# Where a chunk's mask, a few stage slots and one block's logits stand in a gated linear attention with an MLP behind it

## The chip, the cores and the metric

The kernel runs on one core of a Trainium2 chip. The metric is device microseconds of one execution; lower is better. Five runs of the kernel before gave 628.28, 629.21, 629.96, 630.31 and 630.61 us: a median of 629.96 us. One further execution was profiled and took 628.72 us; all rows below come from it.

## The reference

Inputs are q, k, v and f_logit of shape (4, 8, 768, 48), and two weight matrices; all in fp32 but the weights, which arrive as 64-bit floats and are rounded on the core.

```
f = sigmoid(f_logit)
for t in range(768):
    state = f[t][:, None] * state + outer(k[t], v[t])     # 48 x 48 for each batch and head
    y[t]  = q[t] @ state
x = y, as (4*768, 8*48)
h = x @ w_in                                              # 384 -> 2048
out = (h * erf(softplus(h))) @ w_out                      # 2048 -> 384
```

## The kernel before

**Chunks and blocks.** The 4 x 768 tokens are cut into 24 chunks of 128 tokens (numbered from 0; six to a batch), and two chunks make a block of 256 tokens. For each chunk the attention has four stages:

- `stage_d(g)`: one product (line 358) sums the chunk's log gates along time; ScalarE takes two exponentials of it (361 and 364), SyncE sends four small DMAs with the chunk's total decay into `Tall` (line 367, for chunks from 3 on), and VectorE scales q and k (371, 375).
- `stage_t(g)`: q and k are transposed by TensorE (385) and copied out by ScalarE (391, 393).
- `stage_s(g)`: if the chunk is not the last of its batch, `state` makes the products of k and v (433, into the bank `dS`) and VectorE adds the old state (446) and multiplies by `Tall` (449; for a batch's first chunk the one step 442). Then come the score products of k and q (414) and VectorE's mask, one pass of 128 x 1024 (419), whose output is `A`.
- `stage_y(g)`: `y_matmuls` (146) multiplies `A` with v and q with the state that the chunk *before* left; ScalarE copies the result into `xT` (462).

Before a block's stages `prepare` turns its logits into logs: VectorE clips them (335), ScalarE does an Exp and an Ln (339, 340). The Exp and Ln live in another table set than the Tanh of the activation, so a change of set costs ScalarE a table load.

**The MLP.** `hidden` makes the first product (line 515, four tiles of 12 products to a block and group), ScalarE copies it out (522), `activate` runs in steps on ScalarE (152, 155, 487) and VectorE (160, 489). `project` makes the second product by a scheme of seven products for each 2 x 2 of tiles (645) whose sums VectorE prepares (543), and puts the output rows together with a copy (661) and adds (653). `round_piece` turns each of 16 pieces of the weights from 64 bits into fp32: one ScalarE pass (285) and six VectorE passes (287, 291, 296, 300, 305, 310). A piece of `w_in` must be rounded before the products that read it.

**What sets the order.** Every engine runs its instructions in the order in which the program lists them. The list is a loop over turns `it`, one turn for each block; in a turn the generator `slots(it)` yields after each MLP product, and at slot `s` other work is put in: the stages at the slots of the list `at`, steps of the weights' rounding (`weights_step`, one a slot in turn 0 up to slot 42), of the activation, loads, and `prepare`. So a stage's place in `at` decides what stands ahead of it on all five engines. Chunks 0 to 2 run ahead of the loop; turn 0 holds the stages of chunks 3 to 5, turn 1 those of chunks 6 and 7.

**Buffers that bind.** `dS`, the transposes, `ps_d` and `y` share one PSUM pool of two banks (tag `at`): the next of them waits until the last reader of the bank is done. The scores have a bank pair of their own with one buffer.

Of the kernel before, what the change touches and what calls it, by code (L numbers as in the profile page):

```python
# [67 lines left out]
P = 128  # L68
# [3 lines left out]
def kernel(  # L72
# [20 lines left out]
    NCH = S // P  # L93
# [12 lines left out]
    def fixed(name, shape, dtype=FP32, pool=const):  # L106
        return pool.tile(shape, dtype, name=name)
# [58 lines left out]
    fix = main.enter_context(tc.tile_pool(name="fix", bufs=1))  # L166
# [23 lines left out]

    NS, NA = 3, 3
    S_WORDS = NS * NA * FG // 2 * P
    scratch = fixed("scratch", [P, S_WORDS + 7 * DH], pool=fix)
    sums_sb = scratch[:, 0:S_WORDS].rearrange("p (b n j t) -> p b n j t", b=NS, n=NA, j=FG // 2)
    rows_sb = scratch[:, S_WORDS:].rearrange("p (n c) -> p n c", n=7)

    def w_sums(gi):
        return wT[:, gi, :].rearrange("p (n j c) -> p n j c", n=NT, j=FG // 2)
# [197 lines left out]

    def stage_s(g):
        b, c = divmod(g, NCH)
        qT, kT = qTs[g], kTs.pop(g)
        if g in totals:  # L400

            pairs = dps[g % 2][:].rearrange("t (a r) d -> t a (r d)", r=2)
            for a in range(HP):
                nc.tensor.matmul(
                    totals[g][:, a : a + 1], lhsT=pairs[:, a, :], rhs=ident[:, P - 1 : P],
                    start=True, stop=True,
                )
            nc.vector.tensor_copy(out=Tall[:, g, :], in_=totals.pop(g))
        if c < NCH - 1:
            state(g, c)  # L410
        sc = ps_sc.tile([P, 2, HP, P], FP32, name="sc", tag="sc")
        for a in range(HP):
            for r in range(2):
                nc.tensor.matmul(  # L414
                    sc[:, r, a, :], lhsT=kT[rows(r), a, :], rhs=qT[rows(r), a, :],
                    start=True, stop=True,
                )
        A = work1.tile([P, 2, HP, P], FP32, name="A", tag="A")
        nc.vector.tensor_tensor(  # L419
            out=A[:].rearrange("s r a t -> s (r a) t"),  # L420
            in0=sc[:].rearrange("s r a t -> s (r a) t"),
            in1=tri[:].unsqueeze(1).broadcast_to((P, H, P)),
            op=ALU.mult,
        )
        As[g] = A

    def state(g, c):
        dS = ps_at.tile([P, HP, D], FP32, name="dS", tag="at")
# [185 lines left out]
    def project(blk):  # L614


        ops = [ps_moe.tile([P, 2, 512], FP32, name="ops", tag="moe") for _ in range(2)]
        end = blk == n_blocks - 1
        ops.append(ps_sc.tile([P, 2, 512], FP32, name="ops", tag="sc") if end else ops[1])
        place = {n: ops[i][:, j, k * DH : (k + 1) * DH] for n, (i, j, k) in {  # L620
            1: (0, 0, 0), 2: (0, 1, 0), 6: (0, 1, 1), 5: (1, 0, 0), 7: (1, 0, 1), 3: (2, 1, 0), 4: (2, 1, 1),
        }.items()}
        first = [1, 2, 5, 3]

        def pair(n):
            i, j = {2: (0, 1), 5: (1, 0), 3: (2, 1)}[n]
            return ops[i][:, j, 0 : 2 * DH].rearrange("p (n c) -> p n c", n=2)

        def products(gis, ns):
            for gi in gis:  # L630
                gr = groups[blk, gi]
                while gr["sums"] is None:
                    sum_step()
                a11, a12, a21, a22 = blocks(gr["h"])
                w = w_out_sb[:, FG * gi : FG * (gi + 1), :]
                s, t = gr["sums"], w_sums(gi)
                for j in range(2):
                    w1, w2 = w[:, j, :], w[:, 2 + j, :]
                    for n in ns:
                        x, y = {  # L640
                            1: (a11, w1[:, 0:DH]), 2: (a12, w2[:, 0:DH]), 3: (s[2], w2[:, DH:]),
                            4: (a22, t[:, 3, j, :]), 5: (s[0], t[:, 0, j, :]),
                            6: (s[1], t[:, 1, j, :]), 7: (a21, t[:, 2, j, :]),
                        }[n]
                        nc.tensor.matmul(  # L645
                            place[n], lhsT=x[:, j, :], rhs=y,
                            start=(gi == 0 and j == 0 and n in first),
                            stop=(gi == n_g - 1 and j == 1), skip_group_check=True,
                        )
                        yield  # L650

        def plus(out, x, y):
            nc.vector.tensor_tensor(out=out, in0=x, in1=y, op=ALU.add)  # L653

        o = rows_sb
        yield from products((0, 1), (1, 2, 6))
        yield from products((0,), (5, 7, 3, 4))
        to_sum.appendleft(sum_h(groups[blk, 3]))
        yield from products((1,), (5, 7, 3, 4))
        yield from products((2, 3), (1, 2, 6))  # L660
        nc.scalar.copy(out=o[:, 3, :], in_=place[1])  # L661

        plus(o[:, 0:5:4, :], o[:, 3:4, :].broadcast_to((P, 2, DH)), pair(2))
        def fives():

            plus(o[:, 5:7, :], o[:, 4:5, :].broadcast_to((P, 2, DH)), pair(5))

        yield from products((2, 3), (5, 7))
        if end:

            fives()
            plus(o[:, 3, :], o[:, 5, :], place[7])
        yield from products((2, 3), (3, 4))
        if not end:
            fives()
        plus(o[:, 1:3, :], o[:, 5:7, :], pair(3))
        if not end:
            plus(o[:, 3, :], o[:, 5, :], place[7])
        store(blk)

    def chain(*gens):
# [38 lines left out]
    with tc.manual_schedule():  # L720
# [118 lines left out]
        for it in range(n_blocks):  # L839
            gen, n = slots(it)  # L840
            if it == 0:
                todo = [(stage_d, 3), (stage_t, 3), (stage_s, 3), (stage_y, 3), (stage_d, 4), (stage_t, 4),
                        (stage_d, 5), (stage_s, 4), (stage_t, 5), (stage_y, 4)] + stages(2)[4:]
                at = [3, 10, 15, 22, 28, 36, 42, 47, 56, 74, 77, 82, 87, 93]
            else:
                todo = stages(it + 2) if it + 2 < n_blocks else []
                at = [int(3 + (n - 13) / max(1, len(todo)) * i) for i in range(len(todo))]
            if it + 3 < n_blocks:
                prepare_at = at[todo.index((stage_d, (it + 3) * CPB))] - 14
            at, todo = deque(at), deque(todo)  # L850
            for s, _ in enumerate(gen):
                due += (1 if s < 42 else 0.6 if s < 72 else 0.3) if it == 0 else 0.42 if it == 1 else 0.6
                while due >= 1:
                    weights_step()
                    due -= 1
                if s % 6 == 3:
                    load_more()
                if at and s == at[0]:
                    at.popleft()
                    f, g = todo.popleft()  # L860
                    f(g)
                    if f is stage_y:
                        load_to(g + LOOK)
                if it == 0 and s == 17:
                    prepare(2, 0, CPB)
                if it == 0 and s == 9:
                    load_f(6)
                    load_f(7)
                if s == n // 2 and it + 4 < n_blocks:
                    for j in range(CPB):  # L870
                        load_f((it + 4) * CPB + j)
                if it + 3 < n_blocks and s == prepare_at:
                    prepare(it + 3, 0, CPB)
                if it < 2:
                    step = s % 12 == 6 and (it or s >= 24)
                elif it == 2:
                    step = s % 5 in (1, 3)
                else:
                    step = s % 9 in (2, 6)
                if step:  # L880
                    act_step()
                if it == 2:
                    if s == n - 6:
                        to_sum.extend(sum_h(groups[1, gi]) for gi in range(NS))
                    sum_step()
                elif it > 2:
                    if s == n_o and it < n_blocks - 1:
                        to_sum.extend(sum_h(groups[it - 1, gi]) for gi in range(NS))
                    if it == n_blocks - 1 and s % n_o == 40 and s < 2 * n_o:
                        blk = n_blocks - 2 + s // n_o  # L890
                        to_sum.extend(sum_h(groups[blk, gi]) for gi in range(NS))
                    if s < n_o or s % 3 == 0 or it == n_blocks - 1:
                        sum_step()
                if it == n_blocks - 2 and s in (5, 40):
                    next(check)
            assert not todo
# [214 lines left out]
```

## Time and profile before

| what | value |
|---|---|
| median of five runs | 629.96 us |
| the profiled execution | 628.72 us |
| its span (first to last instruction) | 626.9 us |
| TensorE products, share of the span busy | 97% |
| VectorE | 68% |
| ScalarE | 56% |
| GpSimd | 4% |
| TensorE's granted clock, mean | 0.995 |

How to read the rows: times are microseconds from the span's start. PE is TensorE's products and PEld its weight loads, DVE is VectorE, ACT ScalarE, POOL GpSimd, SP SyncE, which issues the DMAs. A row of the timeline gives start, duration, engine, line, operation, output and inputs, shapes, how many instructions it merges, and in brackets how long the engine had idled and what released it. A row of the waits gives the waiting engine and line, the releaser, the sum, how often, and the longest. A row of the windows gives for each engine the busy time in a stretch, then the granted TensorE clock, the DMA engines' share and the rate.

### The profile page before, as it was taken

To read this page: it belongs to the slowest core of one execution; us is meant where nothing else is said; L and a number is where in the kernel's file an instruction comes from. 1 tells how busy PE (TensorE), PEld (TensorE's weight loads), DVE (VectorE), ACT (ScalarE), POOL (GpSimd) and SP (SyncE) were. 2 spreads that over 40 slices of the span, in tenths; PEclk is the share of its full clock that TensorE was granted. 3 is DMA by queue.
4 is the path that set the end of the run, shared out by engine and by line. 5 is a ranking of instruction groups with operands and counts; after the bars stand their busy time and mean duration, and the time that the engine had idled before them with its cause. 6 is when DMAs were issued, how large, how long until landed. Compare 5 with 4: busy or idle time off the path is not lost.

```text
span 626.9 us, 11233 instructions
## 1 busy us (share of the span) xinstructions
PE 605.3 (97%) x4727; PEld 536.0 (85%) x4727; DVE 428.2 (68%) x651; ACT 351.7 (56%) x419; POOL 25.6 (4%) x24
## 2 busy tenths in 40 slices
PE   8896899899999999999999999999999999999996
PEld 7775788788668989889889989988989989989995
DVE  4899997755899576667566675685594764756751
ACT  5345555658763666665855856756747446556300
POOL 0000000000491000000000000000000000000000
PEclk9998999999999999999999999999999999999999
DMA  9999723310211211311221131031000000000000
GB/s 198 244 279 250 198 69 63 64 35 18 51 38 27 66 38 25 78 24 26 51 54 25 27 77 25 14 84 30 15 26 1 2 27 0 15 13 0 26 26 30
DMA packets 120633, 37.02 MB, mean 59 GB/s; under 512 B 112384, under 2 KB 115456, under 8 KB 120576
## 3 DMA queue, kind: packets, MB, share of 16 engines
q1 hardware_dynamic: 118496, 35.84, 24.7%
q8 instruction: 39, 0.64, 0.4%
q10 hardware_dynamic: 2080, 0.39, 0.4%
q14 instruction: 18, 0.15, 0.1%
HBM read 31.46 MB, written 4.72 MB: 58 GB/s over the span
## 4 chain that ended last, share of the span: by engine, by line
PE 80%; DVE 9%; ACT 6%; DMA 2%; issue 1%; SPq 1%; POOL 0%; DVEq 0%; POOLq 0%; ACTq 0%
PE hps L515 34%; PE ops L645 31%; PE y L146 5%; PE sc L414 3%; PE ps_t L385 3%; PE ps_d L358 2%; ACT x L155 1%; DVE e L160 1%; DMA Tall<-dp 1%; DVE scratch L543 1%; PE dS L433 1%; DVE A L419 1%; DMA lt<-in_f_logit_dram 1%; PE busy L348 1%; ACT e L152 1%
## 5 line engine op out<-in xcount | busy, mean ns | idle before, releaser
L515 PE MATMUL hps<-xT,w_in_sb 128*128 128x256 f32 x1152 | 262.1, 382 | 1.4 <-ACT xT L462 1.3
L515 PEld LDWEIGHTS hps<-xT,w_in_sb 128*128 128x128 f32 x1152 | 215.3, 190 | 36.3 <-issue 3.0
L160 DVE SCALAR_TENSOR_TENSOR e<-x,e 128x1024 f32<-128x1024 f32 x96 | 120.9, 1260 | 26.5 <-ACT x L155 26.4
L155 ACT ACTIVATE x<-Hg,serf_bias 128x1024 f32<-128x1024 f32 x88 | 97.7, 1141 | 0.1
L645 PE MATMUL ops<-wT,Hg 128*128 128x192 f32 x352 | 86.8, 328 | 0.0
L152 ACT ACTIVATE e<-Hg 128x1024 f32<-128x1024 f32 x44 | 46.6, 1059 | 63.2 <-DVE Hg L489 62.8
L522 ACT COPY Hg<-hps 128x1024 f32<-128x1024 f32 x44 | 44.5, 1010 | 62.5 <-PE hps L515 62.5
L489 DVE TENSOR_TENSOR Hg<-Hg,e 128x1024 f32<-128x1024 f32 x44 | 54.2, 1233 | 32.3 <-ACT e L487 32.3
L645 PE MATMUL ops<-wT,scratch 128*128 128x192 f32 x320 | 75.1, 326 | 0.7 <-DVE scratch L543 0.7
L645 PE MATMUL ops<-w_out_sb,Hg 128*128 128x192 f32 x352 | 74.3, 328 | 0.0
L645 PEld LDWEIGHTS ops<-wT,Hg 128*128 128x128 f32 x352 | 61.7, 190 | 2.7 <-issue 0.2
L645 PEld LDWEIGHTS ops<-w_out_sb,Hg 128*128 128x128 f32 x352 | 60.0, 190 | 3.7 <-issue 1.2
L653 DVE TENSOR_TENSOR scratch<-scratch,ops 128x384 f32<-128x384 f32 (+1 forms) x44 | 21.3, 502 | 53.2 <-ACT scratch L661 44.3
L645 PEld LDWEIGHTS ops<-wT,scratch 128*128 128x128 f32 x320 | 55.8, 190 | 1.0 <-POOL wT L543 1.0
L487 ACT ACTIVATE e<-e 128x1024 f32<-128x1024 f32 x48 | 50.5, 1051 | 6.2 <-DVE e L160 6.2
L371 DVE TENSOR_TENSOR qd<-qn,dp 128x384 f32<-128x384 f32 x24 | 13.4, 557 | 50.2 <-ACT dp L361 50.2
L146 PE MATMUL y<-A,vt 128*32 128x128 f32 x768 | 36.2, 281 | 7.5 <-DVE A L419 5.8
L146 PEld LDWEIGHTS y<-A,vt 128*32 128x32 f32 x768 | 27.9, 110 | 14.5 <-DVE A L419 5.2
L645 PE MATMUL ops<-w_out_sb,scratch 128*128 128x192 f32 x160 | 39.1, 326 | 0.0
L419 DVE TENSOR_TENSOR A<-sc,tri 128x1024 f32<-128x1024 f32 x24 | 29.4, 1225 | 2.6 <-PE sc L414 2.1
L146 PE MATMUL y<-qT,Mbd 128*32 128x128 f32 x480 | 31.2, 279 | 0.0
L462 ACT COPY xT<-y 128x384 f32<-128x384 f32 x24 | 11.4, 474 | 30.5 <-PE y L146 30.5
(108 smaller groups left out, 647.8 us busy)
## 6 DMA issues: line engine op xcount, KB each, us to landing
lt<-in_f_logit_dram SPq DMA_DIRECT2D x24, 192.0 KB, 3.9
qn<-in_q_dram SPq DMA_DIRECT2D x24, 192.0 KB, 4.2
out_dram<-scratch SPq DMA_DIRECT2D x12, 384.0 KB, 3.6
kn<-in_k_dram SPq DMA_DIRECT2D x23, 192.0 KB, 4.1
vt<-in_v_dram SPq DMA_DIRECT2D x23, 192.0 KB, 3.0
w_out_sb<-in_moe_w_in_dram SPq DMA_DIRECT2D x4, 768.0 KB, 6.5
Hg<-in_moe_w_in_dram SPq DMA_DIRECT2D x4, 768.0 KB, 6.5
Hg<-in_moe_w_out_dram SPq DMA_DIRECT2D x4, 768.0 KB, 5.6
```

Source lines behind the costliest of these rows:

```text
L146: nc.tensor.matmul(y[M * i : M * (i + 1), kt, :], lhsT=terms[n][0], rhs=terms[n][1], start=(n == 0), stop=(n == len(terms) - 1), skip_grou ...
L152: nc.scalar.activation(out=dst[:], in_=h, func=AF.Exp)
L155: nc.scalar.activation(out=dst[:], in_=h, func=AF.Tanh, bias=serf_bias[:, i : i + 1], scale=SERF_KAB[i][0])
L160: nc.vector.scalar_tensor_tensor(out=e[:], in0=x[:], scalar=SERF_KAB[i][2], in1=e[:], op0=ALU.add, op1=ALU.mult)
L385: nc.tensor.transpose(ps[:, a, :], flat[:, a, :], ident[:])
L419: nc.vector.tensor_tensor(out=A[:].rearrange("s r a t -> s (r a) t"), in0=sc[:].rearrange("s r a t -> s (r a) t"), in1=tri[:].unsqueeze(1) ...
L487: nc.scalar.activation(out=e[:], in_=e[:], func=AF.Tanh, scale=SERF_C)
L489: nc.vector.tensor_tensor(out=h, in0=h, in1=e[:], op=ALU.mult)
L515: nc.tensor.matmul(hps[:, j, :], lhsT=w_in_sb[:, kt, ft * P : (ft + 1) * P], rhs=xTs[blk][:, kt, :], start=(kt == 0), stop=(kt == n_k - 1),)
L522: nc.scalar.copy(out=gr["h"], in_=hps[:])
L645: nc.tensor.matmul(place[n], lhsT=x[:, j, :], rhs=y, start=(gi == 0 and j == 0 and n in first), stop=(gi == n_g - 1 and j == 1), skip_grou ...
L653: nc.vector.tensor_tensor(out=out, in0=x, in1=y, op=ALU.add)
```

## The change

- **Mask ahead of the state** for chunks 0 to 5: `stage_s` issues the scores and the mask first and `state` after them. From chunk 6 on the order stays.
- **Turn 0's slots:** `stage_d(4)` goes from slot 28 to 34, `stage_t(4)` from 36 to 42, `stage_d(5)` from 42 to 47, `stage_s(4)` from 47 to 51, `stage_t(5)` from 56 to 60, `stage_d(6)` from 77 to 76, `stage_s(5)` from 82 to 79, `stage_t(6)` from 87 to 88, `stage_y(5)` from 93 to 94; `stage_y(4)` stays at 74.
- **Logits of block 2** (the third): `prepare(2, 0, CPB)` goes from slot 17 to 25 of turn 0. Eight steps of the weights' rounding now stand ahead of it.
- **Turn 1's slots:** 3, 7, 11, 16, 20, 24, 29, 33 become 2, 6, 11, 17, 25, 29, 34, 41. The logits of block 4 hang 14 slots ahead of `stage_d(8)`, and go with it from slot 6 to 11.
- **Two output rows fewer:** the seven products' sums 5 and 6 go into rows 3 and 4 in place of rows of their own, so `scratch` is 2 x 192 words a partition smaller. In the last block the add of product 7 can no longer be done ahead of the last products: it follows the add of products 3 and 4.

```diff
-    scratch = fixed("scratch", [P, S_WORDS + 7 * DH], pool=fix)
+    scratch = fixed("scratch", [P, S_WORDS + 5 * DH], pool=fix)
...
     def stage_s(g):
         b, c = divmod(g, NCH)
+        late = g >= 6
...
-        if c < NCH - 1:
+        if late and c < NCH - 1:
             state(g, c)
         sc = ps_sc.tile([P, 2, HP, P], FP32, name="sc", tag="sc")
...
         As[g] = A
+        if not late and c < NCH - 1:
+            state(g, c)
...
         def fives():
 
-            plus(o[:, 5:7, :], o[:, 4:5, :].broadcast_to((P, 2, DH)), pair(5))
+            plus(o[:, 3:5, :], o[:, 4:5, :].broadcast_to((P, 2, DH)), pair(5))
...
         if end:
 
             fives()
-            plus(o[:, 3, :], o[:, 5, :], place[7])
         yield from products((2, 3), (3, 4))
         if not end:
             fives()
-        plus(o[:, 1:3, :], o[:, 5:7, :], pair(3))
-        if not end:
-            plus(o[:, 3, :], o[:, 5, :], place[7])
+        plus(o[:, 1:3, :], o[:, 3:5, :], pair(3))
+        plus(o[:, 3, :], o[:, 3, :], place[7])
         store(blk)
...
-                at = [3, 10, 15, 22, 28, 36, 42, 47, 56, 74, 77, 82, 87, 93]
+                at = [3, 10, 15, 22, 34, 42, 47, 51, 60, 74, 76, 79, 88, 94]
             else:
                 todo = stages(it + 2) if it + 2 < n_blocks else []
-                at = [int(3 + (n - 13) / max(1, len(todo)) * i) for i in range(len(todo))]
+                at = [n * x // 48 for x in (2, 6, 11, 17, 25, 29, 34, 41)] if it == 1 else [int(3 + (n - 13) / max(1, len(todo)) * i) for i in range(len(todo))]
...
-                if it == 0 and s == 17:
+                if it == 0 and s == 25:
                     prepare(2, 0, CPB)
```

More of the change, by code (lines that the diff above doesn't have):

```diff
@@ L192 @@
     S_WORDS = NS * NA * FG // 2 * P
-    scratch = fixed("scratch", [P, S_WORDS + 7 * DH], pool=fix)
+    scratch = fixed("scratch", [P, S_WORDS + 5 * DH], pool=fix)
     sums_sb = scratch[:, 0:S_WORDS].rearrange("p (b n j t) -> p b n j t", b=NS, n=NA, j=FG // 2)
-    rows_sb = scratch[:, S_WORDS:].rearrange("p (n c) -> p n c", n=7)
+    rows_sb = scratch[:, S_WORDS:].rearrange("p (n c) -> p n c", n=5)
     def w_sums(gi):
```

## The prediction

> **What bounds the kernel now.** I read the page first, then the windows, then the waits of TensorE, then the timeline around the longest of them.
>
> ```profile
> span 626.9 us, 11233 instructions
> PE 605.3 (97%) x4727; PEld 536.0 (85%) x4727; DVE 428.2 (68%) x651; ACT 351.7 (56%) x419; POOL 25.6 (4%) x24
> ...
> 30.00:45.00 15.00, 14.84 (x142) 12.06 (x135) 14.52 (x21) 6.71 (x10) 0.00 (x0) 1.00 1.05 264
> 45.00:50.00 5.00, 0.68 (x4) 0.25 (x2) 2.92 (x7) 0.00 (x0) 0.00 (x0) 1.00 1.15 327
> 50.00:53.00 3.00, 2.50 (x55) 2.43 (x56) 2.97 (x5) 0.19 (x1) 0.00 (x0) 0.64 0.81 271
> 60.00:100.00 40.00, 38.30 (x316) 32.22 (x315) 38.50 (x56) 23.70 (x31) 0.00 (x0) 1.00 0.48 127
> 200.00:560.00 360.00, 360.00 (x2799) 325.49 (x2798) 234.56 (x359) 221.04 (x251) 0.00 (x0) 1.00 0.15 32
> ...
> PE y L146 <- DVE A L419: 5.8, 2, 4.8
> PE ps_t L385 <- DVE Sn L446: 2.7, 2, 1.7
> PE y L146 <- ACT qT L391: 1.7, 1, 1.7
> ```
>
> TensorE is busy without a gap from 200 to 560, so nothing is to be had there: what the change can move lies before 200 and at the very end. In 30 to 100 TensorE and VectorE are both nearly full (14.52 of 15 and 38.50 of 40 for VectorE), because VectorE rounds the weights there; a VectorE that runs late is then as dear as a TensorE that waits. The waits name three places: `y` for the mask (4.8 at 45, 1.0 at 28), a transpose for a state's read (1.7 at 74, 1.0 at 196), `y` for a copy of qT (1.7 at 110).
>
> ```profile
> 45.77 0.34 DVE L446 TENSOR_TENSOR Sn<-dS,Mbd 48x192 f32<-48x192 f32 x1
> 48.07 0.35 DVE L449 TENSOR_TENSOR Mbd<-Sn,Tall 48x192 f32<-48x192 f32 x1 [1.97 <-DMA Tall<-dp]
> 49.22 1.23 DVE L419 TENSOR_TENSOR A<-sc,tri 128x1024 f32<-128x1024 f32 x1
> 50.36 0.95 DVE L305 SCALAR_TENSOR_TENSOR Hg<-Hg 128x768 f32<-128x768 uint32 x1
> 50.50 0.32 PE L146 MATMUL y<-A,vt 128*32 128x128 f32 x4 [4.82 <-DVE A L419]
> 52.22 0.56 DVE L335 TENSOR_SCALAR lt<-lt 128x768 f32<-128x768 f32 x1
> 58.02 0.81 PE L358 MATMUL ps_d<-lt,tri 128*128 128x384 f32 x2
> ...
> 106.39 0.84 ACT L339 ACTIVATE lt<-lt 128x768 f32<-128x768 f32 x1 [2.65 <-DVE lt L335]
> 108.11 1.28 ACT L155 ACT_TABLE_LOAD   x1
> 112.15 0.58 ACT L391 COPY qT<-ps_t 128x512 f32<-128x512 f32 x1
> 112.78 0.43 PE L146 MATMUL y<-A,vt 128*32 128x128 f32 x8 [1.67 <-ACT qT L391]
> ...
> 618.38 0.94 DVE L653 TENSOR_TENSOR scratch<-scratch,ops 128x384 f32<-128x384 f32 x2 [1.70 <-PE ops L645]
> 620.98 0.56 DVE L653 TENSOR_TENSOR scratch<-scratch,ops 128x384 f32<-128x384 f32 x1 [1.66 <-PE ops L645]
> ```
>
> The reader is to see that chunk 3's state waits for the decay's DMA with the mask behind it; that `y(3)` does not need that state (it takes the state of chunk 2); that qT's copy at 112 stands behind block 4's logits; and that the last block ends on one add of 0.56.
>
> **The change, part by part.**
>
> *Chunks 0 to 2, mask first.* Today VectorE works on the state beside the score products. In chunk 1 the state runs 20.27 to 21.76, the scores 20.15 to 21.31, the mask 21.80 to 23.03. Turned round, the scores take the place of the state's products (19.66 to 20.82), the mask runs 20.85 to 22.08 and the state, 1.49 less an overlap of 0.08, to 23.45: VectorE is 0.42 later. Chunk 2 costs the same. In chunk 0 the state is 0.72 long and its bank is freed after it, at 15.0, where the k transpose started at 14.57: 0.3 to 0.4. So VectorE, which feeds the weights to line 515, comes to chunk 3 late by 0.3 + 0.42 + 0.42 = 1.1. Bounds: 0, and 3.5, three whole score products of 1.16 uncovered. I take 1.1 since the rows of chunk 1 give it directly. `y(2)` loses its 1.0 of waiting for the mask, but the products behind it wait for rounded pieces (0.3 and 0.2 at 37.9 and 42.7), so this gain is spent on VectorE's lateness.
>
> *Chunk 3.* The mask starts when the state does today, 45.77 + 1.1 = 46.9, and ends at 48.1. The decay landed at 47.95, so the 1.97 wait is gone: the mask fills it. VectorE's own work between 45.77 and 50.36 is 4.59 - 1.97 = 2.62, so line 305 starts at 46.9 + 2.62 = 49.5 instead of 50.36: VectorE leads by 0.85. TensorE starts `y(3)` at 48.15 instead of 50.50. The half clock also goes: 50 to 53 shows 0.64, and `y(3)` took 50.50 to 53.36, 2.86 where `y(4)` took 1.69. But today's product after it waits for ScalarE's copy of xT till 55.76, behind the logits on ScalarE, so part of that was hidden.
>
> *Logits of block 2 and `stage_d(4)`.* Ahead of line 335 now stand a whole piece (287 at 52.69 to 287 at 57.33: 4.64) and two passes (57.33 to 58.51: 1.18). So it starts at 52.22 - 0.85 + 4.64 + 1.18 = 57.2. Today the end of line 340 comes 2.31 after its start (52.22 to 54.53), so `ps_d(4)` starts at 59.55. TensorE gets there with 35 products of line 515 done, where it has 29 today: six of 0.432, 2.59. It has nothing to do from about 55.6 (48.15, `y` 1.69, copy 0.6, twelve products 5.2): it waits 4.0. Against today at equal work: 59.55 - (58.02 + 2.59) = -1.06.
>
> A new wait of 4.0 may bring the half clock back, as the 4.82 did: by that row it costs 0 to 1.17. I take 0, since in the next step TensorE waits 1.7 again, and what it loses to the clock it would otherwise wait. The Trainium skill, "TensorE: Matmul & The Clock Gate", Part 1, says that after an idle window of about 3.4 us the array runs at half clock until a busy window has passed; that speaks against this new wait, and worked from its figure it is an estimate of up to 1.7 us lost, with which the sum would be +0.5 instead of the one below.
>
> *`stage_t(4)`, `stage_d(5)`, `stage_s(4)`, `stage_t(5)`.* dp(4) follows on ScalarE, and VectorE's scaling (371) now stands behind a full piece after line 335: from 57.65, 4.64 + 2.58 (58.51 to 61.09, line 296 to the end of 305) = 64.85, so the transpose starts at 65.35 with 43 products done; today 62.12 with 37. Equal work: 65.35 - (62.12 + 2.59) = +0.64, so the lead is given back. Then the k transpose of chunk 5 needs chunk 4's state read (the 1.7 wait, second read at 75.85 to 76.21). Ahead of that read now stand the mask (1.15) and two passes more (300 and 305, 1.5): 76.21 + 2.65 - 0.85 = 78.0, with 61 products done against 57 at 76.36 today (four: 1.73). Equal work: 78.1 - 78.09 = 0. So at `y(4)`, slot 74 in both, the opening nets 0.0. Bounds: -1.06 (the lead at `ps_d(4)` is kept) and +2.4 (3.5 late in place of 1.1).
>
> *Queues passed.* On SyncE two transfers of w_out's raw pieces (768 KB, landing after about 5.6) now go ahead of chunk 4's four decay transfers, and block 4's two logit loads ahead of chunk 8's. Chunk 4's decays landed at 63.50 today and are read at 75.49; 12 us cover them. Without that cover each piece would cost about 2.2. GpSimd gets nothing.
>
> *Turn 1.* Today ScalarE does lines 339 and 340 (106.39 to 108.11), a table load of 1.28 and two more passes before qT(7) at 112.15; the `y` of chunk 6 needs the bank that this copy frees. Now the logits stand at slot 11, behind the transposes of the same slot, so the copies come first. The 1.74 of idle goes (110.51 to 112.78, of which 0.53 is the product's own). What is late next is the copy of xT before the products that follow, 0.2. Net -1.55; bounds -1.74 and 0 (the same copy late behind another pass). ScalarE gets two table loads more, 2 x 1.28; it idles 2.65, 1.36, 1.02 and 2.98 between 103 and 122, which covers them; uncovered they cost 2.56 on an engine that has 36 us free in this hundred.
>
> *The end.* The last add becomes two, as at 618.38: 0.94 instead of 0.56, +0.38 on the path to the last store. Bounds 0.27 and 0.41. The smaller scratch and the reuse of rows 3 and 4 change no instruction's size: 0.
>
> Sum: 0.0 - 1.55 + 0.38 = -1.17. The profiled execution, 628.72, becomes 627.55. It lies 1.24 under the median of the runs, so I put the difference on the median: 629.96 - 1.17 = 628.8.
>
> **Rivals.**
> 1. *The opening keeps its gain.* If ScalarE and VectorE serve chunk 4 without the wait of 1.7 for its transpose, the 1.06 stays: 629.96 - 2.23 = 627.7. For it: today this transpose waits for nothing (62.12). Against: VectorE's queue, full in 60 to 100.
> 2. *Turn 1's wait only moves.* Another ScalarE pass stands ahead of the copy: 0.0 + 0.0 + 0.38 gives 630.3. For it: ScalarE's queue is what made the wait; against: 64 of 100 us busy.
> 3. *Slower: the state's bank is held behind the mask.* In chunks 1 and 2 the bank of `dS` comes free 1.23 later each, and transposes, `y` and `ps_d` need it: 2.46 if nothing covers it, 628.8 + 2.46 = 631.25. For it: 1.7 at 74 is just such a wait. Against: in chunk 1 `y` comes at 23.61 and the bank is free at about 23.2. It decides once VectorE reaches chunk 3's mask later than 46.9 + 2.4 = 49.3.
>
> **How the numbers follow.** A measurement of this kernel tells about 0.2%, 1.26 us, from no change. The sum of -1.17 stands just inside that. Chances: forecast 0.51 (0.21 beyond 1.26, 0.29 within, 0.01 slower), rival 1 0.23 (all faster), rival 2 0.12 (all same), rival 3 0.14 (0.13 slower, 0.01 same). Together faster 0.44, same 0.42, slower 0.14. The range, 626.9 to 631.2, runs from rival 1 with turn 1 and the last add at their bounds (627.7 - 0.19 - 0.11 = 627.4), less 0.5 for a median of runs that spread over 2.3, to rival 3, 631.2.
>
> **What would show it.** In the profile after: no wait of 4.8 for the mask, `y(3)` near 48, and a clock of 1.00 in 50 to 53; line 335 near 57 and `ps_d(4)` waiting some 4 us for line 340; a transpose waiting 1.7 near 64 for line 371; no wait of `y` for qT near 111; a last pair of adds of 0.94. I am wrong if VectorE idles again between 30 and 76, if the clock falls after the wait at 56 and `y(4)` starts later than 85.7, or if the early chunks lose more than 1.1.

## The result, and the profile after

The changed kernel took 628.79 us (median of 32 runs, 627.98 to 630.13) beside 629.52 us of the kernel before (median of 55 runs, 628.12 to 631.16). The ratio is 0.9989, with a 95% interval from 0.9984 to 0.9995: 0.7 us faster, between 0.3 and 1.0. The forecast was 628.8 us with a gain of 1.17; the gain is real, inside the 0.2% that I had called no change, and about half a microsecond smaller than the sum. That the two times agree to 0.01 us is luck: the five runs that the forecast stood on had a median of 629.96, 0.44 above the 629.52 of the 55, and the gain by the medians, 0.73, is 0.44 below the 1.17.

Lines moved in the changed file. Line 414 is now 415, 419 is 420, 433 is 436, 446 is 449, 449 is 452, 462 is 465, 515 is 518, 522 is 525, 582 is 585, 645 is 648, 653 is 656; lines up to 391 keep their numbers. The runs below that hold the edit of `stage_s` have the new numbers too. First the page's head and the windows of the opening (start and end, length, busy time and count of PE, PEld, DVE, ACT and POOL, then clock, DMA share, GB/s):

```profile
span 626.2 us, 11238 instructions
...
45.00:50.00 5.00, 3.52 (x65) 2.79 (x63) 4.80 (x9) 0.17 (x1) 0.00 (x0) 1.00 1.11 333
50.00:53.00 3.00, 3.00 (x17) 2.32 (x14) 2.90 (x5) 1.49 (x2) 0.00 (x0) 1.00 1.11 302
53.00:60.00 7.00, 3.09 (x14) 2.37 (x13) 6.79 (x10) 2.10 (x3) 0.00 (x0) 1.00 0.98 262
60.00:65.00 5.00, 5.00 (x16) 3.82 (x15) 4.83 (x8) 4.64 (x7) 0.00 (x0) 0.66 0.58 220
```

TensorE's idle time has moved from 45 to 50 into 53 to 60, and with it the half clock, from 50 to 53 into 60 to 65. VectorE is busy 4.80 of 5 where it was busy 2.92. The waits of TensorE between 30 and 130 in the changed kernel (who waits, for whom, sum, times, longest):

```profile
PE ps_d L358 <- ACT lt L340: 3.9, 1, 3.9
PE y L146 <- DVE A L420: 1.5, 1, 1.5
PE ps_t L385 <- DVE Sn L449: 1.0, 1, 1.0
PE hps L518 <- DVE w_in_sb L310: 0.7, 1, 0.7
PE ps_t L385 <- DVE qd L371: 0.7, 1, 0.7
```

The wait of 4.8 for the mask is 1.5, the wait for qT is gone, and the new wait of 3.9 for the logits is there. The two waits of 0.7 stand at 39.79 and 37.46, at chunk 3, and not at chunk 4. The timeline of the changed kernel at the steps of the prediction:

```profile
47.06 1.22 DVE L420 TENSOR_TENSOR A<-sc,tri 128x1024 f32<-128x1024 f32 x1
48.34 0.42 PE L146 MATMUL y<-A,vt 128*32 128x128 f32 x8 [1.48 <-DVE A L420]
48.58 0.35 DVE L452 TENSOR_TENSOR Mbd<-Sn,Tall 48x192 f32<-48x192 f32 x1
57.28 0.55 DVE L335 TENSOR_SCALAR lt<-lt 128x768 f32<-128x768 f32 x1
59.64 1.33 PE L358 MATMUL ps_d<-lt,tri 128*128 128x384 f32 x2 [3.91 <-ACT lt L340]
60.77 4.93 PE L518 MATMUL hps<-xT,w_in_sb 128*128 128x256 f32 x16
65.53 0.60 PE L385 MATMUL ps_t<-ident,qd 128*128 128x128 f32 x4
78.30 0.63 PE L385 MATMUL ps_t<-ident,kd 128*128 128x128 f32 x4 [1.00 <-DVE Sn L449]
84.91 0.42 PE L146 MATMUL y<-A,vt 128*32 128x128 f32 x8
619.15 0.49 PE L648 MATMUL ops<-wT,Hg 128*128 128x192 f32 x2
619.67 0.94 DVE L656 TENSOR_TENSOR scratch<-scratch,ops 128x384 f32<-128x384 f32 x2 [2.05 <-PE ops L648]
620.64 0.37 SPq L585 DMA_DIRECT2D out_dram<-scratch  x1
```

The last products and the last store of the kernel before, beside the last three of these rows:

```profile
620.45 0.49 PE L645 MATMUL ops<-wT,Hg 128*128 128x192 f32 x2
621.56 0.37 SPq L582 DMA_DIRECT2D out_dram<-scratch  x1
```

| step | before | forecast | after |
|---|---|---|---|
| chunk 3's mask starts | 49.22 | 46.9 | 47.06 |
| `y(3)` | 50.50 | 48.15 | 48.34 |
| line 335 of block 2 | 52.22 | 57.2 | 57.28 |
| `ps_d(4)`, and its wait | 58.02, 0 | 59.55, 4.0 | 59.64, 3.91 |
| transposes of chunk 4 | 62.12 | 65.35 | 65.53 |
| k transpose of chunk 5 | 76.36 | 78.0 | 78.30 |
| `y(4)` | 84.69 | 84.7 | 84.91 |
| last add (after: the last pair) | 620.98 | | 619.67 |

The last store is issued at 620.64 where it was 621.56: 0.92 earlier, made of +0.22 at `y(4)`, -1.52 from there to the start of the last products, and +0.38 behind it. So the pair of profiles comes near the forecast; the medians of many runs give less. That remainder, and which of the parts earns, is what the experiments were for.

### The profile page after: what moved, and what is told of

It reads as the page before. It is cut to its first block, busy times and chain, and to the rows that moved or that the text cites. A ratio compares the mean times of both kernels' runs of the same rounds, so it can differ in the third digit from the quotient of the medians.

```text
span 626.2 us, 11238 instructions
## 1 busy us (share of the span) xinstructions
PE 606.3 (97%) x4727; PEld 535.3 (85%) x4727; DVE 429.3 (69%) x651; ACT 354.3 (57%) x421; POOL 25.7 (4%) x24
## 4 chain that ended last, share of the span: by engine, by line
PE 79%; DVE 12%; ACT 4%; DMA 2%; issue 2%; SPq 0%; DVEq 0%; ACTq 0%
PE hps L518 33%; PE ops L648 31%; PE y L146 5%; PE sc L415 3%; PE ps_t L385 3%; PE ps_d L358 2%; DVE e L160 1%; DVE scratch L546 1%; ACT x L155 1%; PE dS L436 1%; DMA qn<-in_q_dram 1%; DVE A L420 1%; DVE w_in_sb L310 1%; DVE w_in_sb L296 1%; ACT e L152 1%
```

## The experiments

My theory: the opening is set by VectorE's list, the change removes VectorE's wait for chunk 3's decay and pays for that in the early chunks and at chunk 4, net 0; turn 1 gains 1.55; the end costs 0.38. Against it stood the three rivals of the prediction: that the opening keeps a gain, that turn 1's wait only moves, and that the state's bank is held behind the mask and costs 2.5.

### One part at a time: mask, slots of turn 0, slots of turn 1, last adds

**The mask alone.** The kernel before with

```diff
+        late = g >= 6
...
-        if c < NCH - 1:
+        if late and c < NCH - 1:
             state(g, c)
...
+        if not late and c < NCH - 1:
+            state(g, c)
```

> The kernel before with the mask first in chunks 0 to 5 and nothing else moved. By the terms of the prediction: VectorE comes to chunk 3 late by 1.1, y(3) starts near 48.2 instead of 50.5 and the wait of 4.8 is gone; but block 2's logits stay at slot 17, so on ScalarE the copy of xT behind y(3) still stands behind lines 339 and 340 and comes at about 55.24 - 0.85 = 54.4. TensorE waits there some 4 instead of 1.3: the wait moves, it does not go. At chunk 5's k transpose the mask (1.15) stands ahead of the state's read: +0.3. Sum -0.85 to +0.3, 'same'. Rival 3 (banks held behind the mask, 1.23 each in chunks 1 and 2): +2.5, slower, and transposes or y that wait before 40. If the opening kept its gain by the mask alone: -1 or better.

Measured: 1.0011 of before, interval 1.0000 to 1.0022, so +0.7 us. That is above the expected -0.85 to +0.3, though the interval reaches down to 0. The timeline shows the wait moved, as expected, and more:

```profile
48.16 0.42 PE L146 MATMUL y<-A,vt 128*32 128x128 f32 x8 [1.49 <-DVE A L420]
54.71 0.46 ACT L465 COPY xT<-y 128x384 f32<-128x384 f32 x1
55.22 4.64 PE L518 MATMUL hps<-xT,w_in_sb 128*128 128x256 f32 x10 [4.67 <-ACT xT L465]
61.16 0.56 DVE L371 TENSOR_TENSOR qd<-qn,dp 128x384 f32<-128x384 f32 x1 [0.62 <-ACT dp L361]
```

`y(3)` comes 2.3 earlier and nothing is gained by it: the copy of xT stands behind block 2's logits on ScalarE. The ten products after the wait run mostly at half clock (a granted clock of 0.50 in 54 to 58), 4.64 where ten take 2.43 in the kernel before. So `ps_d(4)` comes late, at 59.65, and VectorE waits 0.62 for its exponential. Here the half clock reached the engine that sets the pace.

**The slots of turn 0 and the logits' place alone.**

```diff
-                at = [3, 10, 15, 22, 28, 36, 42, 47, 56, 74, 77, 82, 87, 93]
+                at = [3, 10, 15, 22, 34, 42, 47, 51, 60, 74, 76, 79, 88, 94]
...
-                if it == 0 and s == 17:
+                if it == 0 and s == 25:
```

> The kernel before with the slots of turn 0 and the place of block 2's logits (17 to 25) as in the changed kernel, the state still ahead of the mask. By the terms of the prediction: the waits of 4.8 and 1.0 of y stay; the logits come at about 57.2 + 0.85 = 58.0, xT's copy of chunk 3 is no longer behind them (its wait of 1.3 goes), ps_d(4) at about 60.4 after 35 products, a wait of 1 to 2, and the transpose of chunk 4 waits 1.7 for VectorE's scaling. Equal work at y(4): 0 within 0.6. If the slots by themselves bring the opening's gain: -1; if the later transpose decides: +0.6.

Measured: 0.9993 (0.9984 to 1.0002), -0.4 us. Line 335 came at 57.79 and `ps_d(4)` at 60.16, near the expectation, but without the expected wait of the products for the logits (only their weight load waited, 0.39); the transposes of chunk 4 waited 1.47. `y(4)` started at 84.22. The slots are worth little by themselves.

**The slots of turn 1 alone.**

```diff
-                at = [int(3 + (n - 13) / max(1, len(todo)) * i) for i in range(len(todo))]
+                at = [n * x // 48 for x in (2, 6, 11, 17, 25, 29, 34, 41)] if it == 1 else [int(3 + (n - 13) / max(1, len(todo)) * i) for i in range(len(todo))]
```

> The kernel before with the slots of turn 1 alone. My term: the wait of 1.7 of y for qT near 111 goes, -1.55 on the whole time (0.9975). Rival 2 (another pass of ScalarE stands ahead of the copy): a wait of about 1.7 elsewhere between 100 and 130, 0.

Measured: 0.9964 (0.9950 to 0.9977), -2.3 us with an interval from -3.1 to -1.4. The rows are sharper than the times: from `y(4)` to the start of the last pair of products it is 534.01 us, where the three other kernels with this opening and the old turn 1 have 535.76 (before), 535.67 (last adds alone) and 535.77 (the early decay, below). So turn 1 is worth 1.7. No wait of `y` is left between 100 and 130, and the copy of xT that I had expected to be 0.2 late is not late. Rival 2 is out.

**The last adds alone.** The new order of the adds and the smaller `scratch`, as in the diff of the change.

> The kernel before with the new order of the last adds alone. My term: the last add of 0.56 becomes a pair of 0.94, +0.38 (1.0006), bounds 0.27 and 0.41; nothing else differs. If the last store hides it: 0.

Measured: 1.0007 (0.9998 to 1.0017), +0.4 us. From the start of the last products to the issue of the last store it is 1.49 here, in the changed kernel and in its second profile; it is 1.10 to 1.11 in the kernel before and in every profiled variant of it with the old adds. The term is +0.38, and no store hides it.

This run's profile shows something else as well. Its opening is the kernel before, instruction for instruction:

```profile
45.25 0.34 DVE L446 TENSOR_TENSOR Sn<-dS,Mbd 48x192 f32<-48x192 f32 x1
49.47 0.35 DVE L449 TENSOR_TENSOR Mbd<-Sn,Tall 48x192 f32<-48x192 f32 x1 [3.87 <-DMA Tall<-dp]
53.61 0.56 DVE L335 TENSOR_SCALAR lt<-lt 128x768 f32<-128x768 f32 x1
86.07 0.43 PE L146 MATMUL y<-A,vt 128*32 128x128 f32 x8
```

The decay came 1.4 later than in the profile of before (used at 49.47 for 48.07), VectorE waited 3.87 instead of 1.97, and `y(4)` came 1.38 later. In the run of turn 1 alone it was used at 48.99 and `y(4)` came at 85.58. From the use of the decay to `y(4)` it is 36.62, 36.59 and 36.60 in the three: with the old order the opening follows this one landing, one for one, and the landing moves by 1.4 between executions. The profile of before was an early one, and so was its time, 0.8 under the median of the 55 runs.

What moves is the time at which SyncE comes to issue the four transfers. First the profile of before, then this one:

```profile
40.95 2.49 SPq L367 DMA_DIRECT2D Tall<-dp  x4
```

```profile
42.19 2.64 SPq L367 DMA_DIRECT2D Tall<-dp  x4
```

In the eight profiles in which VectorE waited for these transfers of SyncE, the first issue lies between 40.72 and 42.34, and the use comes 7.11 to 7.35 after it.

### The opening as a whole

The first two parts together, without turn 1 and the last adds, in two runs.

> The kernel before with the mask first in chunks 0 to 5 and the new slots of turn 0 and block 2's logits: the whole opening, without turn 1 and the last adds. My term: 0.0, bounds -1.06 and +2.4, so 1.000. What the runs so far leave for it: the changed kernel stands at -0.7, turn 1 alone at -2.3 (bounds -3.1 and -1.4), the last adds alone at +0.4, so the opening would have to cost some +1.1 (+0.3 to +1.9). If the parts simply add, mask alone +0.7 and slots alone -0.4 make +0.3.

> The kernel with the mask and the slots of turn 0 alone once more, for a second profile: its first gave y(4) at 84.66 and was the fastest of its twelve times (628.95, median 629.88). Expected y(4) near 85.6. By the decay: a wait for it behind the mask of about 0.9. By the clock: half clock after the wait of 3.9 that the next wait does not hide.

Measured: 1.0012 (1.0003 to 1.0020), and 1.0003 (0.9992 to 1.0014) when it was run again. Both profiles have `y(4)` where the profile of before has it, 84.66 and 84.69 against 84.69, and no wait for the decay. From `y(4)` to the last products it is 535.97 and 535.98, 0.2 to 0.3 more than the 535.65 to 535.77 with the old slots. The slots alone have 536.04 and the mask alone 535.65, so this comes from the slots; it is there by `y(6)`, which starts 28.28 and 28.30 after `y(4)` here and 28.04 to 28.11 after it with the old slots. This is the opening's cost that the rows show, and my sum did not have it, since it ended at `y(4)`. The second run was to show an execution with a late `y(4)` and did not. By the rows the opening costs 0.2, by the times 0.2 to 0.75; what the rest is, no profile here shows.

The changed kernel itself, run and profiled again:

> The changed kernel once more, for a second profile: its first profiled execution was among the fastest of its runs. If the spread of its executions is the landing of chunk 3's decay, VectorE waits for it behind the mask in a slower execution (0.3 to 1.2, as in two of the runs with the mask first), and y(4) is later than 84.9 by that much. If it is the clock: y(4) is later by up to 1.7 with the same landing.

It took 0.9986 of before (0.9972 to 1.0000), and its profile was a late one:

```profile
47.03 1.22 DVE L420 TENSOR_TENSOR A<-sc,tri 128x1024 f32<-128x1024 f32 x1
49.60 0.35 DVE L452 TENSOR_TENSOR Mbd<-Sn,Tall 48x192 f32<-48x192 f32 x1 [1.08 <-DMA Tall<-dp]
58.30 0.56 DVE L335 TENSOR_SCALAR lt<-lt 128x768 f32<-128x768 f32 x1
85.91 0.43 PE L146 MATMUL y<-A,vt 128*32 128x128 f32 x8
```

It is the decay: with the same start of the mask, VectorE waits 1.08 behind it, and `y(4)` is 1.00 later than in the first profile. So the mask does not free the opening from the landing. It covers 1.2 of the wait, and VectorE has come to chunk 3 1.1 later, so the landing binds again from about 48.5 on. From the landing's use to `y(4)` it is now 36.31, against 36.6 before: in a late execution the new order is 0.3 ahead, in one like the profile of before level. Where the decay is used before 48.0, as it was at 47.94 in one of the profiles, the old order is ahead, by an estimate from these two distances.

### Where the mask pays and where it costs

> The changed kernel with the mask first in chunks 3 to 5 only; in chunks 0 to 2 the state comes first as before. By my term for chunks 0 to 2 VectorE comes to chunk 3 1.1 earlier: mask at 45.9, y(3) at 47.2, line 335 at 56.1, ps_d(4) at 58.5, and at most 1.1 is won on the changed kernel: 0.997 of before. y(2) waits 1.0 for its mask again. If the lead is given back at chunk 4's state (the mask of 1.15 ahead of the read for chunk 5's k transpose): as the changed kernel, 0.9989. Rival 3 (banks held behind the mask in chunks 1 and 2): a gain of 2.5, 0.995.

The edit to the changed kernel is `late = g >= 6 or g < 3`. Measured: 0.9969 (0.9959 to 0.9979), 1.3 us better than the changed kernel's ratio. VectorE starts on chunk 3 at 46.84 to 47.06 in the five profiles with the mask first in chunks 0 to 2, and at 45.25 to 46.19 in the nine with the state first there. The means are 46.93 and 45.80: the early chunks cost 1.13, which the prediction had as 1.1. Rival 3's 2.5 is not there. The gain is in the times; the one profile of this run does not show it, since its decay came late: VectorE waited 1.23 for it behind the mask, line 335 came at 57.53 and not at 56.1, and `y(4)` at 85.12, 0.2 later than in the changed kernel's first profile.

> The changed kernel with the mask first in chunk 3 alone, where the state waits for its decay; chunks 0 to 2, 4 and 5 as before. As the run beside it, and the mask no longer stands ahead of chunk 4's state: the wait of chunk 5's k transpose (1.0 in the changed kernel) goes too. By my terms 1.1 for the early chunks and up to 1.0 for the transpose: 0.9956 to 0.997 of before. If the early chunks' order costs nothing: 0.9973 at best.

The edit is `late = g != 3`. Measured: 0.9955 (0.9943 to 0.9968), 2.8 us faster than before and 2.1 better than the changed kernel's ratio. The wait of the k transpose of chunk 5 for chunk 4's state is gone, since the mask no longer stands ahead of that state: VectorE's second read of it starts 19.37 after line 335, where it is 20.51 in the changed kernel.

> As the run beside it, with the last adds of the kernel before: 0.38 less, 0.995 to 0.9964 of before. Meant to beat both kernels.

Measured: 0.9959 (0.9947 to 0.9971). The times can't tell it from the run above; the rows show 1.10 from the last products to the store instead of 1.50, so the 0.4 is there; this execution waited 0.28 for the decay, where the other did not, and had `y(4)` 0.45 later (83.12 for 82.67).

Thirteen of the fourteen profiles can be laid on one rule. Between VectorE's clip of block 2's logits (line 335) and `y(4)` there is a fixed time that depends on the list alone:

| slots of turn 0 | chunk 4 | line 335 to `y(4)` | profiles |
|---|---|---|---|
| old | state first | 32.44 to 32.47 | 4 |
| new | mask first | 27.59 to 27.63 | 5 |
| new | state first | 26.43 to 26.48 | 4 |

(The fourteenth, the mask alone, has 34.38: the old slots' 32.45, the mask's 1.15 and the 0.62 of waiting for the late exponential make 34.22 of it.) Within a row the spread is 0.05 at most, while TensorE's longest wait in this stretch goes from 1.5 to 4.2 within the last row and reaches 5.1 in the one above. And between 30 and 90 VectorE is never idle for more than 0.15 in any of the profiles, but for the waits for the decay, this 0.62 and one of 0.34. So VectorE sets the opening up to the transposes of chunk 4; behind them, in the last row, TensorE has no wait up to `y(4)` either (16.00 busy of 16 between 66 and 82). The mask ahead of chunk 4's state costs 27.6 - 26.45 = 1.15.

### No mask moved, but the decay earlier

If what counts is VectorE's wait, then taking away what it waits for must do as much as hiding it:

```diff
-                nc.sync.dma_start(
+                (nc.scalar if g == 3 else nc.sync).dma_start(
                     out=Tall[:, g, a : a + 1],
```

> The kernel before with one thing changed: chunk 3's four decay transfers are issued on ScalarE's queue, right after dp(3) (done at 34.65), where on SyncE's queue they are issued at 40.95 behind the loads. State still ahead of the mask, all slots old. If VectorE's idle for this decay is what the opening pays (1.97, 2.18, 2.84 and 3.87 in four profiles of this opening), all behind it moves up by that much: y(3) near 48.5, y(4) near 82.7, -2.0 to -2.8 on the time, 0.9955 to 0.997. If a later wait (xT behind the logits, the k transpose for the state's read, a piece's transfer) takes it: 0, 1.000.

On the kernel before, this one line measured 0.9973 (0.9961 to 0.9986), -1.7 us: a little less than expected, and by these two values 2.5 times what the whole change earned.

```profile
34.40 3.23 ACTq L367 DMA_DIRECT2D Tall<-dp  x4
46.29 0.35 DVE L449 TENSOR_TENSOR Mbd<-Sn,Tall 48x192 f32<-48x192 f32 x1
48.72 0.66 PE L146 MATMUL y<-A,vt 128*32 128x128 f32 x8 [2.89 <-DVE A L419]
50.44 0.55 DVE L335 TENSOR_SCALAR lt<-lt 128x768 f32<-128x768 f32 x1
82.89 0.43 PE L146 MATMUL y<-A,vt 128*32 128x128 f32 x8
```

The four transfers are issued at 34.40 where SyncE issued them at 40.95, VectorE reads the decay at 46.29 without a wait, and `y(4)` comes at 82.89.

> The changed kernel with the state first in every chunk, as before, and chunk 3's decay on ScalarE's queue: no mask is moved. If what counts is that VectorE does not idle for the decay, and the mask's place only serves that, then y(3) starts at about 48.5, line 335 at 56.2 and y(4) at 83.8 as in the run with the mask first in chunk 3 alone: 0.9955. If y(3)'s own earlier start is what counts, it is 1.2 later there: 0.9974. If the early decay lands too late all the same: VectorE idles 2 to 3 again and the time is that of before less turn 1, 0.998.

The changed kernel with `late = True` (the state first everywhere) and the same line: 0.9945 (0.9929 to 0.9961), 626.20 us beside 628.98. It is the best of all ratios, though its interval overlaps that of the run with the mask first in chunk 3 alone, 0.9943 to 0.9968. (The expectation put `y(4)` at 83.8; that run had it at 82.67.) First the rows of that run, then of this one:

```profile
47.21 0.43 PE L146 MATMUL y<-A,vt 128*32 128x128 f32 x8 [1.36 <-DVE A L420]
56.19 0.55 DVE L335 TENSOR_SCALAR lt<-lt 128x768 f32<-128x768 f32 x1
58.55 1.65 PE L358 MATMUL ps_d<-lt,tri 128*128 128x384 f32 x2 [3.95 <-ACT lt L340]
59.99 4.37 PE L518 MATMUL hps<-xT,w_in_sb 128*128 128x256 f32 x16
64.37 0.66 PE L385 MATMUL ps_t<-ident,qd 128*128 128x128 f32 x4
82.67 0.43 PE L146 MATMUL y<-A,vt 128*32 128x128 f32 x8
```

```profile
48.62 0.42 PE L146 MATMUL y<-A,vt 128*32 128x128 f32 x8 [2.89 <-DVE A L420]
56.06 0.55 DVE L335 TENSOR_SCALAR lt<-lt 128x768 f32<-128x768 f32 x1
58.42 0.91 PE L358 MATMUL ps_d<-lt,tri 128*128 128x384 f32 x2 [2.41 <-ACT lt L340]
59.17 3.62 PE L518 MATMUL hps<-xT,w_in_sb 128*128 128x256 f32 x16
64.27 0.66 PE L385 MATMUL ps_t<-ident,qd 128*128 128x128 f32 x4 [1.48 <-DVE qd L371]
82.51 0.42 PE L146 MATMUL y<-A,vt 128*32 128x128 f32 x8
```

`y(3)` starts 1.41 later and `y(4)` 0.16 earlier: an early `y(3)` is worth nothing in itself. And the pair prices the half clock. In the first the long wait ends in it: the two products of `ps_d` and the sixteen behind them take 0.84 + 0.75 = 1.59 longer than the 0.81 and 3.62 of the kernel before. In the second the clock stays at 1.00, and the time is spent waiting 1.48 for VectorE's scaling. Both reach the transposes within 0.10.

## Why the prediction was right, and where it was off

- **What bounds the opening.** I read "nearly full VectorE, so a late VectorE is as dear as a waiting TensorE". The runs make it sharper: up to chunk 4's transposes VectorE sets it, and an earlier `y(3)` is worth nothing by itself (1.41 later in the best run, and `y(4)` 0.16 earlier).
- **Chunks 0 to 2, +1.1 on VectorE:** 1.13 by the means of fourteen profiles, 1.29 in the first pair (45.77 to 47.06). The working has a slip of 0.04 (22.08 + 1.49 - 0.08 is 23.49), which the sum's rounding hides. The k transpose of chunk 0 waits 0.36 for its bank (0.3 to 0.4 forecast). The gain at `y(2)` was spent as forecast: the products behind it wait 0.7 for rounded pieces, where they waited 0.2, and chunk 3's transposes wait 0.7 for VectorE's scaling, where they did not wait.
- **Chunk 3:** the mask fills the wait, and `y(3)` and line 335 come within 0.2 of the forecast. That holds where the decay lands by about 48.5. I took one landing, 47.95, for a constant; it moves by 1.4 between executions. In the changed kernel's second profile two of my signs of being wrong are there: VectorE idles 1.08 between 30 and 76, and `y(4)`, after a fall of the clock, starts at 85.91, later than 85.7. The cause of both is the landing, which I had not let vary.
- **`ps_d(4)` and the half clock.** The wait of 3.91 and the half clock both came; the clock lost 0.52 + 1.31 = 1.83 in the changed kernel. The page of the Trainium skill "TensorE: Matmul & The Clock Gate", Part 1, from which I had an estimate of up to 1.7 lost, is close in size here. The sum by that estimate, +0.5, was wrong and the term 0 was right, for the reason given: the forecast wait of 1.7 of chunk 4's transposes for VectorE is gone (their products do not wait, their weight load waits 0.18), and they started 0.18 later than forecast. What the clock took, they would have waited.
- **The lead given back at chunk 4:** right, and now priced. The mask ahead of chunk 4's state costs 1.15; I had the same amount in the working (the mask's 1.15 in the 78.0).
- **Turn 1, -1.55:** -1.7 by the rows. The 0.2 for a late copy of xT was not paid.
- **The end, +0.38:** +0.38.
- **The step that was missing** is one that the text did not write down: after `y(4)` the opening was taken to cost nothing more. The new slots of turn 0 cost 0.2 to 0.3 between `y(4)` and `y(6)`; those of `stage_d(6)` to `stage_y(5)` lie there, but no run moves them alone. With the rows' terms the sum is 0.0 + 0.2 - 1.7 + 0.38 = -1.1. The timed gain is -0.69, between -1.0 and -0.3, so some 0.4 are still not accounted for. The opening's own runs, +0.75 and +0.2, point there, but their intervals reach from -0.5 to +1.3; where these 0.4 lie, and whether they are more than noise, stays open.
- **The rivals.** Rival 1 had a right core in the wrong version: the opening can gain 2, as in the two runs with the new slots and without the mask at chunks 0 to 2 and 4 (`y(4)` at 82.67 and 82.51 for 84.69). Rival 2 and rival 3 did not happen.

## What to carry to other kernels

Find the engine whose list fixes the stage, by measuring a distance between two of its instructions in several variants: where it is the same to 0.05 while another engine's waits go from 1.5 to 4.2, those waits are free, and so is a half clock behind them, as long as the slowed products are done by the time the first engine is. With the mask alone they were not, and the first engine waited 0.62. Reordering work to hide a late transfer pays only at the place where that transfer is late; applied to the neighbours it cost 1.1 and 1.15 here and ate what it earned. Before hiding a small transfer, see what it is queued behind: another issuing queue gave 1.7 us for one line.

## What was not expected of the hardware

- **The issue of a small DMA moves the whole kernel.** The 0.5 KB decay transfers of chunk 3 were used between 47.94 and 49.47 in four profiles that are alike up to there, and in the three with the old slots `y(4)` moved with them one for one. From issue to use they took nearly the same time in each; what moved was the issue, behind SyncE's loads. What delays these loads more in one execution than in another no row here shows. Nor does this seem to be the whole spread of the times: with the decay early, twelve runs still lie between 626.66 and 629.26. The Trainium skill, "DMA: Bandwidth & Descriptors", "Issuing engines are not separate DMA queues", says that issuing on several engines saves only the sequencer's time, usually small beside the transfer. Here it was not small: 6.55 us earlier (40.95 to 34.40), where from issue to landing the median of the four was 5.8 on SyncE's queue and 4.4 on ScalarE's, since the transfers stood behind loads that SyncE had not yet issued. On ScalarE's queue the four issues took 3.23.
- **The half clock and the length of the wait.** Every wait of TensorE of 3.9 or more in these profiles was followed by the half clock. In the seven profiles with the long wait for the logits the loss in the products behind it went from 1.59 (wait 3.95) to 2.99 (wait 5.10, mask from chunk 3 on), with 1.82 after a wait of 4.95: the length of the wait does not tell it. A wait of 2.89 was followed by it in one execution and not in another. These are the windows of the early decay on the kernel before, then on the changed one:

```profile
50.00:53.00 3.00, 2.67 (x41) 1.78 (x32) 2.93 (x5) 1.94 (x3) 0.00 (x0) 0.65 0.95 305
```

```profile
50.00:53.00 3.00, 3.00 (x27) 2.20 (x17) 2.90 (x5) 1.49 (x2) 0.00 (x0) 1.00 0.95 324
```

The Trainium skill, "TensorE: Matmul & The Clock Gate", Part 1, gives an idle window of about 3.4 us; a wait shorter than that was enough once here (2.89, with a clock of 0.65 behind it), and the loss of 2.99 is above the 1.7 estimated from that window.
